# Attention steps of a fused kernel: transposes, drains and products with v one step later, other buffer counts, a smaller warm-up tile

## The chip, the cores and the metric

One core of one Trainium2 chip runs the whole program. The metric is the device time of one execution in microseconds. The kernel before takes 725.25 us, the median of three runs (724.98 to 725.36).

## The reference

Three parts follow one another, all in float32:

```python
# attention: B=2, H=8, S=576, D=64, scale = 1/8
cum = np.cumsum(np.maximum(s, 0.0), axis=-1)
bias = -(cum[:, :, :, None] - cum[:, :, None, :])
scores = np.where(causal, -1e9, scale * q @ k.T + np.minimum(bias, 0.0))
scores = scores - np.max(scores, axis=-1, keepdims=True)
attn = np.exp(scores)
attn = attn / (np.sum(attn, axis=-1, keepdims=True) + 1e-09)
x = (attn @ v) laid out as [B*S, H*D]            # 1152 x 512

# experts: E=4, F=1024
p = domain_probs / (domain_probs.sum(-1, keepdims=True) + 1e-09)
out = sum(p[:, e:e+1] * (np.maximum(x @ w1[e], 0.0) @ w2[e]) for e in range(E))

# gated layer, 1536 wide
y = ((out @ w_a) * (out @ w_b)) @ w_out
```

## The kernel before

**The whole.** Nearly all products are made of three matmuls (line 281): each operand is split into a high part and a rest (`xh`, `xl`, `wh`, `wl`), and high by high, rest by high and high by rest add up in one PSUM tile. The program has three stretches. In the first 30 us it does the attention of the first 256 tokens (the head, lines 787 to 865), eight heads one after another; while it waits for data, `keep_warm` (line 732) gives TensorE matmuls on a tile of ones, `lull`, whose result nobody reads (line 736). From 30 to about 194 us the attention of the other tokens runs beside expert 0 on the first 256 tokens (plain float32 matmuls, line 1037) and beside expert 1. After that come the other experts and the gated layer, up to 724 us.

**The attention pipeline.** The rest of the attention is 24 jobs: three groups of tokens, `GROUPS` (0,2,5), (1,0,3) and (1,3,5), eight heads each. A job has one tile of 128 queries for each index in its range; `sc_6_2_4` is the scores of head 6, of the group that begins at tile 2, for tile 4 (a number behind it in the queues below tells buffers apart). The second and third group are batch 1's and begin at tiles 0 and 3, so `av_3_0` is head 3 of the second group. `seq` lists all (job, tile) pairs. Step n of `attn_work` (line 939) issues one phase for each of several pairs, so that a pair goes through the phases in successive steps:

- scores of pair n (`st_scores`, L627 and L628, PSUM tag `sc`, two buffers; more than 512 keys take two pieces);
- softmax of pair n-1 (`st_softmax`): VectorE adds the mask and finds the row's extreme, out of PSUM into a tile `e` (L638); ScalarE takes the exponential (L651). `e` has five buffers;
- division of pair n-2 (`st_norm`): ScalarE L657, VectorE's reciprocal L658, GpSimd's product L659;
- transposes of pair n-3 on TensorE (`st_transpose`, L670), 128 keys each, into PSUM tag `tr`, two buffers of up to four blocks. A tile with five blocks takes a buffer with four and then one with the fifth;
- drain of pair n-3 (`st_evac`): ScalarE copies `tr` to `eh` (L685), then VectorE writes the rest to `el` (L686). A `tr` buffer is free when L686 has read it;
- when the last tile of a job is at n-4, its product with v (`st_av`, L702, PSUM tag `av`, one buffer): `eh` and `el` by `vs`. ScalarE (L719) and VectorE (L720) take the result out, and every second head GpSimd helps to split it into `xh`, `xl`.

The same steps load the next jobs' q, k, v (SyncE queues, L587 to L607) and prepare them (`prep_job`: `qh` on ScalarE, `qb` on VectorE L595, `ks` on ScalarE and GpSimd; `prep_v`: `vs`, two buffers).

**What sets the order.** The products of the experts are called in units, and `advance()` between them calls as many attention steps as a pace wants: for each group of tokens `lead` has the step by which the group must be through, `ends` (the last step of the group plus five), and the time of the stage by which it must be, 15 us ahead of the stage that reads the group's tokens. The written order is only a wish: a scheduler places every instruction in its engine's queue, and manual dependencies (`passed`) hold the experts' matmuls behind the attention steps. On the engine the queue is then fixed.

**Buffers.** Pool `h` holds the experts' hidden tiles (`hh`, `hl`, eleven buffers of each tag), pool `e` the tiles of the softmax.

Of the kernel before, what the change touches and what calls it, by code (L numbers as in the profile page):

```python
# [10 lines left out]
BF16 = mybir.dt.bfloat16  # L11
# [9 lines left out]
P = 128  # L21
NC = DM // P
SL = 512
# [14 lines left out]
GROUPS = [(0, 0, 2), (0, 2, 5), (1, 0, 3), (1, 3, 5)]  # L38
# [21 lines left out]
def fused_kernel(ctx, tc, qk0, v0, qT, kT, v, s, dp, w1, w2, wa, wb, wo, out):  # L60
    nc = tc.nc
# [21 lines left out]
    def open_pools(c, names):  # L83
        for name, bufs in names:
            pools[name] = c.enter_context(tc.tile_pool(name=name, bufs=bufs))
# [430 lines left out]


    actx = ExitStack()
    open_pools(actx, [("h", 11), ("raw", 3)])
    fix_p = actx.enter_context(tc.tile_pool(name="fix", bufs=1))  # L520
    causal = fix_p.tile([P, S], F32, name="causal")

# [1 line left out]
    qbs = [fix_p.tile([RB, 3 * P], F32R, name=f"qb{m}") for m in range(2)]  # L524
    rw_p = actx.enter_context(tc.tile_pool(name="rw", bufs=1))
    io_p = actx.enter_context(tc.tile_pool(name="io", bufs=2))
    e_p = actx.enter_context(tc.tile_pool(name="e", bufs=5))
    et_p = actx.enter_context(tc.tile_pool(name="et", bufs=2))
    st_p = actx.enter_context(tc.tile_pool(name="st", bufs=8))
    x_p = actx.enter_context(tc.tile_pool(name="x", bufs=1))  # L530
# [20 lines left out]
    def in_order(ins):  # L551
        return tc.keep_in_program_order(ins)
# [27 lines left out]
    def load_job(j):  # L580
        b, h = j.b, j.h
        j.qh = io_p.tile([P, j.nq], F32R, tag="qh", name=f"qh{j.nm}")
        j.qb = qbs[(j.h + 1) % 2]
        j.qr = rw_p.tile([P, j.nq], F32, tag="qr", name=f"qr{j.nm}")
        j.kr = rw_p.tile([P, j.nk], F32, tag="kr", name=f"kr{j.nm}")
        j.kb = io_p.tile([RB, j.nk], F32R, tag="kb", name=f"kb{j.nm}")
        queued(nc.sync.dma_start(out=j.qr, in_=qT[b, h, :, j.q0 : j.q1]))  # L587
        queued(nc.sync.dma_start(out=j.kr, in_=kT[b, h, :, : j.nk]))
        queued(nc.sync.dma_start(out=j.kb[D:, :].bitcast(F32), in_=ckD[:, PLACE[j.gi], h, : j.nk]))

    def prep_job(j):
        j.t = {}
        j.ks = io_p.tile([P, j.nk], F32R, tag="ks", name=f"ks{j.nm}")
        nc.scalar.activation(out=j.qh, in_=j.qr, func=AF.Copy, scale=SCALE)
        nc.vector.scalar_tensor_tensor(  # L595
            out=j.qb[:D, : j.nq], in0=j.qr[:D], scalar=SCALE, in1=j.qh[:D].bitcast(F32),
            op0=ALU.mult, op1=ALU.subtract,
        )
        nc.scalar.activation(out=j.ks, in_=j.kr, func=AF.Copy)
        queued(nc.sync.dma_start(out=j.kb[:D].bitcast(F32), in_=j.ks[:D].bitcast(F32)))  # L600
        nc.gpsimd.tensor_tensor(
            out=j.ks[D:, :], in0=j.kr[D:, :], in1=j.ks[D:, :].bitcast(F32), op=ALU.subtract
        )
# [11 lines left out]
    def st_enter(j, i):  # L615
        j.t[i] = Job()
        j.t[i].n = j.tiles[i][0] + P
# [36 lines left out]
    def st_norm(j, i):  # L654
        t = j.t[i]
        r = st_p.tile([P, 1], F32, tag="r", name="r")
        nc.scalar.activation(out=t.l, in_=t.l, func=AF.Copy, bias=1e-9)  # L657
        nc.vector.reciprocal(out=r, in_=t.l)  # L658
        nc.gpsimd.tensor_scalar(  # L659
            out=t.e, in0=t.e, scalar1=r, scalar2=1.0, op0=ALU.mult, op1=ALU.mult  # L660
        )
# [64 lines left out]

    lull = fix_p.tile([P, SL], BF16, name="lull")
    nc.gpsimd.memset(lull, 1.0)  # L730
    lull_ps = ps_m.tile([P, SL], F32, tag="mm", name="lullps")

    def keep_warm(n):

        for _ in range(n):
            in_order(nc.tensor.matmul(lull_ps, lhsT=lull[:, :P], rhs=lull, start=True, stop=True))  # L736

    sc = e_p.tile([NS, S], F32, tag="e", name="s_sb")
    ones = e_p.tile([P, S], F32, tag="e", name="ones")
# [15 lines left out]
    early[0] = False  # L755

    keep_warm(12)
    nc.vector.memset(ones, 1.0)
    nc.gpsimd.memset(sel_, 0.0)
# [167 lines left out]
    seq = [(j, i) for j in jobs for i in range(j.i0, j.i1)]  # L927
    state = {"n": 0}

    def at(n):  # L930
        return seq[n] if 0 <= n < len(seq) else None
# [7 lines left out]
    def attn_work(n):  # L939
        state["n"] += 1  # L940
        passed.append([])

        if x := at(n):
            j, i = x
            if i == j.i0:
                k = jobs.index(j)
                if k + 1 < len(jobs):
                    prep_job(jobs[k + 1])
                if k + 2 < len(jobs):
                    load_job(jobs[k + 2])  # L950
            st_enter(j, i)
        if x := at(n - 3):
            st_transpose(*x)
        if x := at(n):
            st_scores(*x)
        if x := at(n - 2):
            st_norm(*x)
        if x := at(n - 1):
            st_softmax(*x)
        if x := at(n - 4):  # L960
            j, i = x
            if i == j.i1 - 1:
                st_av(j)
        if x := at(n - 3):
            st_evac(*x)
        if x := at(n):
            j, i = x
            if i == j.i0:
                prep_v(j)
                k = jobs.index(j)  # L970
                if k + 1 < len(jobs):
                    load_v(jobs[k + 1])


    ends = [0] + [
        max(n for n, (j, i) in enumerate(seq) if j.gi == g) + 5 for g in range(1, len(GROUPS))
    ]

    late_ps = []
# [287 lines left out]
    n = [k for k, u in enumerate(after) if u[0] == ("w1", halves[1][1])][-1]  # L1267
# [12 lines left out]
    for n in range(len(seq) + 12):  # L1280
        x = at(n)
# [108 lines left out]
```

## Time and profile before

| | |
|---|---|
| median of three runs | 725.25 us (724.98 to 725.36) |
| the profiled execution's own time | 725.65 us |
| its span in the profile | 723.9 us |
| TensorE busy | 710.9 us (98%) |
| VectorE, ScalarE, GpSimd busy | 512.9, 323.5, 398.8 us |
| granted clock of TensorE | 1.000 of full speed |
| chain that ended last | TensorE 76%, VectorE 9%, GpSimd 5%, ScalarE 4% |

The span is what the profiler sees of the program from its first to its last instruction; the execution's own time is 1.75 us longer. TensorE is the fullest engine. Its busy time counts pipelined matmuls, whose ends are modelled, so a place is read from the starts of neighbouring matmuls and from the idle time that stands in brackets, with what released the engine.

### The profile page before, as it was taken

To read this page: it belongs to the slowest core of one execution; us is meant where nothing else is said; L and a number is where in the kernel's file an instruction comes from. 1 tells how busy PE (TensorE), PEld (TensorE's weight loads), DVE (VectorE), ACT (ScalarE), POOL (GpSimd) and SP (SyncE) were. 2 spreads that over 40 slices of the span, in tenths; PEclk is the share of its full clock that TensorE was granted. 3 is DMA by queue.
4 is the path that set the end of the run, shared out by engine and by line. 5 is a ranking of instruction groups with operands and counts; after the bars stand their busy time and mean duration, and the time that the engine had idled before them with its cause. 6 is when DMAs were issued, how large, how long until landed. Compare 5 with 4: busy or idle time off the path is not lost.

```text
span 723.9 us, 10979 instructions
## 1 busy us (share of the span) xinstructions
PE 710.9 (98%) x3884; PEld 620.9 (86%) x3886; DVE 512.9 (71%) x1060; ACT 323.5 (45%) x722; POOL 398.8 (55%) x329
## 2 busy tenths in 40 slices
PE   9999999999999999999999999999999999999998
PEld 5886798999899888888888888887999888888886
DVE  5586878767686866765655666589973969787674
ACT  3597899877434333331223123334544424243410
POOL 5476866655235544430333057687277879788600
PEclk9999999999999999999999999999999999999999
DMA  8665434442111211120111021222021222212003
GB/s 328 209 176 141 126 88 119 124 120 62 57 41 58 89 58 58 59 65 24 58 59 47 13 88 59 88 87 88 30 87 59 88 88 83 92 60 88 1 0 131
DMA packets 33724, 61.42 MB, mean 85 GB/s; under 512 B 3285, under 2 KB 17525, under 8 KB 33669
## 3 DMA queue, kind: packets, MB, share of 16 engines
q1 hardware_dynamic: 33189, 59.61, 26.6%
q10 hardware_dynamic: 480, 1.11, 0.4%
q8 instruction: 31, 0.51, 0.3%
q14 instruction: 24, 0.20, 0.1%
HBM read 55.11 MB, written 2.58 MB: 80 GB/s over the span
## 4 chain that ended last, share of the span: by engine, by line
PE 76%; DVE 9%; POOL 5%; issue 4%; ACT 4%; DMA 3%; SPq 0%; POOLq 0%; ACTq 0%; DVEq 0%
PE ps L281 34%; PE psq L281 24%; PE pst L281 6%; PE av L702 2%; PE tr L670 2%; POOL wl L81 2%; PE ps L1037 2%; DMA raw<-in_wo 1%; DVE el L686 1%; DVE tp L174 1%; PE lullps L736 1%; ACT e L651 1%; DVE h2l L81 1%; DVE tp L170 1%; POOL tp L162 1%
## 5 line engine op out<-in xcount | busy, mean ns | idle before, releaser
L281 PE MATMUL ps<-wh,h2h 128*128 128x512 f32 (+1 forms) x334 | 131.1, 392 | 0.6 <-ACT h2h L80 0.6
L281 PE MATMUL ps<-wl,h2h 128*128 128x512 f32 (+1 forms) x334 | 129.9, 389 | 0.0
L81 POOL TENSOR_TENSOR wl<-raw,wh 128x1024 fp32r<-128x1024 f32 x24 | 58.2, 2433 | 129.0 <-ACT wh L80 98.6
L281 PE MATMUL ps<-wh,h2l 128*128 128x512 f32 (+1 forms) x334 | 125.6, 390 | 0.0
L335 DVE SCALAR_TENSOR_TENSOR acc<-ps,pr,acc 128x512 f32<-128x512 f32 x111 | 82.3, 746 | 41.1 <-PE ps L281 40.4
L281 PE MATMUL psq<-xh,wh 128*128 128x448 f32 (+1 forms) x224 | 81.7, 365 | 0.1
L281 PE MATMUL psq<-xh,wl 128*128 128x448 f32 (+1 forms) x224 | 81.4, 363 | 0.0
L281 PE MATMUL psq<-xl,wh 128*128 128x448 f32 (+1 forms) x224 | 81.3, 363 | 0.0
L281 PEld LDWEIGHTS ps<-wh,h2l 128*128 128x128 f32 x334 | 62.7, 188 | 13.2
L281 PEld LDWEIGHTS ps<-wh,h2h 128*128 128x128 f32 x334 | 62.8, 188 | 13.0 <-ACT h2h L80 1.3
L346 ACT ACTIVATE h2h<-psq 128x448 fp32r<-128x448 f32 (+1 forms) x56 | 29.5, 530 | 95.5 <-PE psq L281 76.4
L281 PEld LDWEIGHTS ps<-wl,h2h 128*128 128x128 f32 x334 | 62.8, 188 | 10.9
L81 POOL TENSOR_TENSOR wl<-sums,wh 128x1024 fp32r<-128x1024 f32 x24 | 58.3, 2427 | 4.9 <-ACT wh L80 4.9
L80 ACT ACTIVATE wh<-raw 128x1024 fp32r<-128x1024 f32 x24 | 25.5, 1062 | 69.6 <-PE ps L281 53.0
L281 PE MATMUL psq<-tqh,wh 128*128 128x448 f32 x144 | 53.0, 368 | 1.3 <-DVE h2l L81 0.9
L281 PE MATMUL psq<-tql,wh 128*128 128x448 f32 x144 | 52.6, 365 | 0.0
L281 PE MATMUL psq<-tqh,wl 128*128 128x448 f32 x144 | 52.5, 364 | 0.0
L162 POOL TENSOR_SCALAR tp<-tp 128x512 f32<-128x512 f32 x24 | 48.0, 2017 | 5.8 <-ACT tp L161 5.8
L686 DVE TENSOR_TENSOR el<-tr,eh 128x512 fp32r<-128x512 f32 (+5 forms) x80 | 38.3, 484 | 16.4 <-ACT eh L685 15.6
L659 POOL TENSOR_SCALAR e<-e,r 128x448 f32<-128x448 f32 (+4 forms) x64 | 37.8, 595 | 17.5 <-DVE r L658 12.9
L281 PEld LDWEIGHTS psq<-xh,wh 128*128 128x128 f32 x224 | 42.1, 188 | 4.3 <-ACT s L445 0.9
L281 PEld LDWEIGHTS psq<-xl,wh 128*128 128x128 f32 x224 | 42.1, 188 | 3.5
(205 smaller groups left out, 1877.2 us busy)
## 6 DMA issues: line engine op xcount, KB each, us to landing
raw<-in_w SPq DMA_DIRECT2D x32, 512.0 KB
raw<-in_wa SPq DMA_DIRECT2D x12, 512.0 KB
raw<-in_wb SPq DMA_DIRECT2D x12, 512.0 KB
raw<-in_wo SPq DMA_DIRECT2D x12, 512.0 KB
kr<-in_kT SPq DMA_DIRECT2D x16, 288.0 KB
w<-in_w SPq DMA_DIRECT2D x8, 512.0 KB
vr<-in_v SPq DMA_DIRECT2D x16, 160.0 KB
kb<-ks SPq DMA_DIRECT2D x16, 144.0 KB
```

Source lines behind the costliest of these rows:

```text
L80: nc.scalar.activation(out=hi, in_=src, func=AF.Copy)
L81: lo_eng.tensor_tensor(out=lo, in0=src, in1=hi.bitcast(F32), op=ALU.subtract)
L162: nc.gpsimd.tensor_scalar(out=t.bitcast(F32), in0=t.bitcast(F32), scalar1=2.0**-15, scalar2=GMAX, op0=ALU.max, op1=ALU.min,)
L170: nc.vector.scalar_tensor_tensor(out=t, in0=lo, scalar=29, in1=t, op0=ALU.logical_shift_right, op1=ALU.bitwise_or,)
L281: ins = nc.tensor.matmul(ps, lhsT=l, rhs=r, start=first and k == 0, stop=last and k == 2, skip_group_check=more)
L335: nc.vector.scalar_tensor_tensor(out=dst, in0=ps, scalar=share, in1=dst, op0=ALU.mult, op1=ALU.add)
L346: nc.scalar.activation(out=hh, in_=src, func=AF.Relu)
L659: nc.gpsimd.tensor_scalar(out=t.e, in0=t.e, scalar1=r, scalar2=1.0, op0=ALU.mult, op1=ALU.mult)
L670: ins = nc.tensor.transpose(ps[:, c - c0, :], t.e[:, k0 : k0 + P], ident)
L686: nc.vector.tensor_tensor(out=j.el[:, c0:c1, x], in0=src, in1=hi.bitcast(F32), op=ALU.subtract)
L702: ins = nc.tensor.matmul(ps[:, o:], lhsT=j.vs[:, c, :], rhs=e[:, c, o:], start=(m == 0), stop=(m == len(mms) - 1),)
L1037: ins = nc.tensor.matmul(ps, lhsT=w, rhs=x, start=start, stop=stop)
```

## The change

It does five things:

1. `st_transpose` and `st_evac` are called for pair n-4, no longer n-3; `st_av` for a job whose last tile is n-5, no longer n-4. Scores, softmax and division stay where they were.
2. `ends` counts six steps behind a group's last pair, no longer five.
3. `e` has six buffers for five.
4. `h` has ten buffers for eleven.
5. `lull` is 128 columns wide for 512; the matmul reads these 128 columns four times through a broadcast, so it has the same shape (128 x 512) as before.

```diff
-    open_pools(actx, [("h", 11), ("raw", 3)])
+    open_pools(actx, [("h", 10), ("raw", 3)])
...
-    e_p = actx.enter_context(tc.tile_pool(name="e", bufs=5))
+    e_p = actx.enter_context(tc.tile_pool(name="e", bufs=6))
...
-    lull = fix_p.tile([P, SL], BF16, name="lull")
+    lull = fix_p.tile([P, P], BF16, name="lull")
...
-            in_order(nc.tensor.matmul(lull_ps, lhsT=lull[:, :P], rhs=lull, start=True, stop=True))
+            in_order(nc.tensor.matmul(
+                lull_ps.rearrange("p (a b) -> p a b", b=P), lhsT=lull,
+                rhs=lull.unsqueeze(1).broadcast_to([P, SL // P, P]), start=True, stop=True,
+            ))
...
-        if x := at(n - 3):
+        if x := at(n - 4):
             st_transpose(*x)
...
-        if x := at(n - 4):
+        if x := at(n - 5):
             j, i = x
             if i == j.i1 - 1:
                 st_av(j)
-        if x := at(n - 3):
+        if x := at(n - 4):
             st_evac(*x)
...
-        max(n for n, (j, i) in enumerate(seq) if j.gi == g) + 5 for g in range(1, len(GROUPS))
+        max(n for n, (j, i) in enumerate(seq) if j.gi == g) + 6 for g in range(1, len(GROUPS))
```

Below line 735 the changed file's lines are three higher for the same code (L1037 is L1040). From the end of the attention on, TensorE's queue is the same row for row. Inside the attention the scheduler has laid it out anew, and three places show how.

TensorE at the first head of the first group, before. `tr_0_2_3` fills one `tr` buffer, `tr_0_2_4` the other with four blocks, and the fifth block needs the first one back. The matmuls into `ps` are expert 0's first layer, the `sc` rows the next head's scores.

```order
L670 MATMUL tr_0_2_3_573<-ident,e_0_2_3_520 128x128 x4
L1037 MATMUL ps_633<-ckr,w_117 128x256 x3
L627 MATMUL sc_1_2_4_611<-ks_1_2_468,qh_1_2_448 128x320
L628 MATMUL sc_1_2_4_611<-kb_1_2_451,qb_83 128x320
L670 MATMUL tr_0_2_4_604<-ident,e_0_2_4_551 128x128 x4
L627 MATMUL sc_1_2_4_614<-ks_1_2_468,qh_1_2_448 128x256
L628 MATMUL sc_1_2_4_614<-kb_1_2_451,qb_83 128x256
L670 MATMUL tr_0_2_4_609<-ident,e_0_2_4_551 128x128
```

The same place after the change:

```order
L670 MATMUL tr_0_2_3_596<-ident,e_0_2_3_519 128x128 x4
L1040 MATMUL ps_665<-ckr,w_117 128x256
L627 MATMUL sc_1_2_4_601<-ks_1_2_468,qh_1_2_448 128x320
L628 MATMUL sc_1_2_4_601<-kb_1_2_451,qb_83 128x320
L627 MATMUL sc_1_2_4_604<-ks_1_2_468,qh_1_2_448 128x256
L628 MATMUL sc_1_2_4_604<-kb_1_2_451,qb_83 128x256
L1040 MATMUL ps_665<-ckr,w_117 128x256
L1040 MATMUL ps_714<-ckr,w_117 128x256 x3
L670 MATMUL tr_0_2_4_633<-ident,e_0_2_4_547 128x128 x4
L627 MATMUL sc_2_2_2_640<-ks_2_2_527,qh_2_2_474 128x320
L628 MATMUL sc_2_2_2_640<-kb_2_2_477,qb_84 128x320
L670 MATMUL tr_0_2_4_638<-ident,e_0_2_4_547 128x128
```

Between the two fills of that buffer there stand now five matmuls of expert 0 for three, and the scores of `sc_2_2_2`, which were behind this place, have come in front of the fifth block.

TensorE at head 6 of the same group, before: the rows that lead to head 7's first transposes, `tr_7_2_2`, which take the buffer that `tr_6_2_4` with four blocks had. Ahead of these rows stand those four transposes, the two matmuls of `sc_0_0_2`, the fifth block's transpose and six more L281.

```order
L281 MATMUL ps_1427<-xh,wh 128x256
L281 MATMUL ps_1427<-xl,wh 128x256
L281 MATMUL ps_1427<-xh,wl 128x256
L627 MATMUL sc_1_0_0_1505<-ks_1_0_1365,qh_1_0_1231 128x128
L628 MATMUL sc_1_0_0_1505<-kb_1_0_1234,qb_83 128x128
L702 MATMUL av_6_2_1396<-eh_6_2_1271,vs_6_2_1160 128x320
L670 MATMUL tr_7_2_2_1378<-ident,e_7_2_2_1309 128x128 x3
```

After the change:

```order
L670 MATMUL tr_6_2_4_1364<-ident,e_6_2_4_1230 128x128 x4
L628 MATMUL sc_0_0_2_1451<-kb_0_0_1107,qb_84 128x320
L627 MATMUL sc_1_0_0_1488<-ks_1_0_1351,qh_1_0_1209 128x128
L628 MATMUL sc_1_0_0_1488<-kb_1_0_1212,qb_83 128x128
L670 MATMUL tr_6_2_4_1369<-ident,e_6_2_4_1230 128x128
L281 MATMUL ps_1439<-xh,wh 128x256
L281 MATMUL ps_1439<-xl,wh 128x256
L281 MATMUL ps_1439<-xh,wl 128x256
L627 MATMUL sc_1_0_1_1522<-ks_1_0_1351,qh_1_0_1209 128x192
L628 MATMUL sc_1_0_1_1522<-kb_1_0_1212,qb_83 128x192
L702 MATMUL av_6_2_1413<-eh_6_2_1294,vs_6_2_1136 128x320
L670 MATMUL tr_7_2_2_1397<-ident,e_7_2_2_1274 128x128 x3
```

The nine L281 between the two uses have become three; the scores of `sc_1_0_0` and `sc_1_0_1` have come between instead.

VectorE's queue there, before, around the drain of `tr_6_2_4`:

```order
L638 ISA e_0_0_1_1473,mn<-sc_0_0_1_1436,causal 128x192
L638 ISA mn 128x1
L686 TENSOR_TENSOR el_6_2_1272<-tr_6_2_4_1336,eh_6_2_1271 128x4x128
L595 SCALAR_TENSOR_TENSOR qb_84<-qr_2_0_1372,qh_2_0_1371 64x320
L658 RECIPROCAL r<-l 128x1
L686 TENSOR_TENSOR el_6_2_1272<-tr_6_2_4_1341,eh_6_2_1271 128x128
```

and after:

```order
L658 RECIPROCAL r<-l 128x1
L638 ISA e_0_0_2_1495,mn<-sc_0_0_2_1451,causal 128x320
L638 ISA mn 128x1
L595 SCALAR_TENSOR_TENSOR qb_84<-qr_2_0_1358,qh_2_0_1357 64x320
L686 TENSOR_TENSOR el_6_2_1295<-tr_6_2_4_1364,eh_6_2_1294 128x4x128
L686 TENSOR_TENSOR el_6_2_1295<-tr_6_2_4_1369,eh_6_2_1294 128x128
```

The preparation `qb` stood behind the drain of the four blocks and now stands ahead of it, and the softmax in front is that of `sc_0_0_2` (320 keys), no longer of `sc_0_0_1` (192 keys).

TensorE at head 3 of the second group, where `av_3_0` needs what the last tile's transposes, `tr_3_0_2`, leave in `eh` and `el`, before:

```order
L670 MATMUL tr_3_0_2_1887<-ident,e_3_0_2_1836 128x128 x3
L281 MATMUL ps_1789<-wh,hh 128x512
L281 MATMUL ps_1789<-wl,hh 128x512
L281 MATMUL ps_1789<-wh,hl 128x512
L281 MATMUL ps_1789<-wh,hh 128x512
L281 MATMUL ps_1789<-wl,hh 128x512
L281 MATMUL ps_1789<-wh,hl 128x512
L627 MATMUL sc_5_0_2_1982<-ks_5_0_1814,qh_5_0_1715 128x320
L628 MATMUL sc_5_0_2_1982<-kb_5_0_1718,qb_83 128x320
L670 MATMUL tr_4_0_0_1918<-ident,e_4_0_0_1874 128x128
L627 MATMUL sc_6_0_0_2016<-ks_6_0_1905,qh_6_0_1820 128x128
L628 MATMUL sc_6_0_0_2016<-kb_6_0_1823,qb_84 128x128
```

After the change:

```order
L627 MATMUL sc_5_0_2_1973<-ks_5_0_1805,qh_5_0_1698 128x320
L628 MATMUL sc_5_0_2_1973<-kb_5_0_1701,qb_83 128x320
L670 MATMUL tr_3_0_2_1909<-ident,e_3_0_2_1829 128x128 x3
L627 MATMUL sc_6_0_0_2004<-ks_6_0_1896,qh_6_0_1811 128x128
L628 MATMUL sc_6_0_0_2004<-kb_6_0_1814,qb_84 128x128
L670 MATMUL tr_4_0_0_1935<-ident,e_4_0_0_1853 128x128
L627 MATMUL sc_6_0_1_2028<-ks_6_0_1896,qh_6_0_1811 128x192
L628 MATMUL sc_6_0_1_2028<-kb_6_0_1814,qb_84 128x192
L702 MATMUL av_3_0_1949<-eh_3_0_1869,vs_3_0_1723 128x320
L627 MATMUL sc_6_0_2_2066<-ks_6_0_1896,qh_6_0_1811 128x320
L628 MATMUL sc_6_0_2_2066<-kb_6_0_1814,qb_84 128x320
L702 MATMUL av_3_0_1949<-el_3_0_1870,vs_3_0_1723 128x320
```

Before, `av_3_0` came in the row behind these; after, the product with `eh` is the ninth row and that with `el` the last. Six L281 of expert 1 stood between the transposes and the product with v; none does now, and scores have taken part of their place.

## Rows read from the trace of the kernel before

**Rows 1.** Two stretches: us, length, then busy us (instructions) by engine, granted clock, DMA share
```profile
30.00:194.00 164.00, 157.69 (x1052) 139.41 (x1051) 119.78 (x392) 134.13 (x412) 105.06 (x131) 1.00 0.40 112
194.00:724.00 530.00, 524.76 (x2673) 461.33 (x2671) 377.21 (x608) 176.38 (x279) 278.51 (x161) 1.00 0.20 65
```

**Rows 2.** TensorE's waits, 30 to 195 us: releaser, total us, times, longest
```profile
PE tr L670 <- DVE el L686: 2.1, 6, 0.6
PE tr L670 <- DVE r L658: 1.3, 2, 0.7
PE av L702 <- DVE el L686: 1.2, 3, 0.8
PE sc L627 <- DVE mn L638: 1.0, 1, 1.0
PE av L702 <- ACT eh L685: 0.4, 1, 0.4
```

**Rows 3.** Timeline near 50 us: start, duration, what, [idle before <-releaser]
```profile
49.79 0.67 DVE L686 TENSOR_TENSOR el<-tr,eh 128x512 fp32r<-128x512 f32 x1
...
50.39 0.14 DVE L658 RECIPROCAL r<-l 128x1 f32<-128x1 f32 x1
...
50.60 0.30 PE L670 MATMUL tr<-ident,e 128*128 128x128 f32 x1 [0.70 <-DVE r L658]
```

**Rows 4.** Timeline near 182 us: one block of four transposes and its drain
```profile
182.11 0.63 PE L670 MATMUL tr<-ident,e 128*128 128x128 f32 x4 [0.63 <-DVE r L658]
...
182.50 0.36 PE L702 MATMUL av<-el,vs 128*128 128x256 f32 x1
...
182.78 0.60 ACT L685 ACTIVATE eh<-tr 128x512 fp32r<-128x512 f32 x1 [0.22 <-PE tr L670]
...
183.41 0.69 DVE L686 TENSOR_TENSOR el<-tr,eh 128x512 fp32r<-128x512 f32 x1 [0.65 <-ACT eh L685]
```

**Rows 5.** TensorE's timeline: five of its waits in their places
```profile
41.72 0.33 PE L670 MATMUL tr<-ident,e 128*128 128x128 f32 x1 [0.59 <-DVE el L686]
...
71.34 0.39 PE L627 MATMUL sc<-ks,qh 128*128 128x256 f32 x1 [0.98 <-DVE mn L638]
...
84.74 0.63 PE L670 MATMUL tr<-ident,e 128*128 128x128 f32 x4 [0.35 <-DVE el L686]
...
86.05 0.33 PE L670 MATMUL tr<-ident,e 128*128 128x128 f32 x1 [0.26 <-DVE el L686]
...
112.37 0.41 PE L702 MATMUL av<-el,vs 128*128 128x320 f32 x1 [0.81 <-DVE el L686]
```

**Rows 6.** Groups by form, 30 to 195 us: busy us, mean ns | idle before
```profile
L638 DVE CUSTOM_DVE_ANT_0 e<-sc,causal 128x320 f32<-128x320 f32 x32 | 15.4, 480 | 2.5 <-PE sc L628 1.8 <-PE tr L670 0.4
...
L595 DVE SCALAR_TENSOR_TENSOR qb<-qr,qh 64x320 fp32r<-64x320 f32 x8 | 5.3, 663 | 0.0
...
L686 DVE TENSOR_TENSOR el<-tr,eh 128x384 fp32r<-128x384 f32 x8 | 4.5, 557 | 1.7 <-ACT eh L685 1.6
...
L685 ACT ACTIVATE eh<-tr 128x384 fp32r<-128x384 f32 x8 | 3.8, 476 | 0.0
```

**Rows 7.** Line 595: duration in ns, least, median, longest; first and last start, forms
```profile
L595 DVE SCALAR_TENSOR_TENSOR qb<-qr,qh x24: 411/547/1569, 26.6 to 171.3; 64x384 fp32r<-64x384 f32 x8, 64x320 fp32r<-64x320 f32 x8, 64x256 fp32r<-64x256 f32 x8
```

**Rows 8.** Chain of waits: start, duration, run of matmuls on TensorE
```profile
55.70 2.58 PE ps L1037 x6
...
86.38 1.75 PE ps L281 x15
```

**Rows 9.** Timeline of the first 7 us
```profile
0.80 0.52 POOL L730 MEMSET lull<- 128x512 bf16 x1 [0.29 <-POOLq L1376]
...
1.38 5.30 PE L736 MATMUL lullps<-lull 128*128 128x512 bf16 x12 [1.38 <-POOL self L759]
...
1.81 0.20 POOL masks.py:197 MEMSET ident<- 128x128 f32 x1
...
6.61 0.46 PE L797 MATMUL sc<-cb,sel 40*128 40x128 f32 x1
```

## The prediction

> **What bounds it now.** I read the table by stretches first, then TensorE's waits between 30 and 195 us, then the timeline around each of those waits, then durations by form. The reader is to see that TensorE runs without a break where the kernel spends most of its time: 524.76 of 530 us behind the attention, at the full granted clock [rows 1], and its queue there is unchanged. So a shift that the attention makes is carried to the end, whole. In the 164 us of the attention TensorE is busy 157.69 [rows 1], and its waits for another engine sum to 6.0 us [rows 2]. That is all that a better pipeline could give; what a worse one costs has no such bound.
>
> Which waits are they? The list names L658, the reciprocal, for 1.3 us. That reading is wrong, and the timeline shows it: the fifth block's transpose starts at 50.60, the `el` of the block that had its buffer ends at 49.79 + 0.67 = 50.46, and the reciprocal at 50.39 merely ended last [rows 3]. So 3.4 us are waits for a `tr` buffer to be drained, 1.6 us (1.2 and 0.4) waits of the product with v for `el` and `eh`, and 1.0 us one wait of scores for an `sc` buffer [rows 2]. Not one waits for a normalised `e`. The extra step puts more work between division and transposes, where no wait was; the drain and the product move by the same step, so their distance is set anew only by the order of the queues.
>
> **The measure of a drain.** Four transposes start at 182.11 and the next matmul at 182.50, so a block takes 0.1; `eh` starts at 182.78, `el` at 183.41 and ends 0.69 later, at 184.10 [rows 4]. With 0.14 from there to the next transpose [rows 3] a buffer is ready 1.75 us after its last transpose. Work of TensorE between two uses of a buffer that falls short of 1.75 is waited for. Split matmuls run back to back at 1.75 / 15 = 0.117 for 256 columns, so 0.06, 0.09 and 0.145 for 128, 192 and 320; plain float32 matmuls leave two records each, 2.58 / 6 = 0.43 a record of 512 columns, so 0.43 for an instruction of 256 [rows 8].
>
> **Part by part.**
>
> *The small tile.* Its fill takes 0.52, and the matmuls start behind it at 1.38; the identity's, of as many bytes as the new tile, takes 0.20 [rows 9]. The scores follow the last warm-up matmul, whose run ends at 6.68 [rows 9]. So the head starts 0.32 earlier at most, and at least not at all if a load sets it. I take **-0.2** (0 to -0.32), nearer the row that shows scores right behind the run.
>
> *Buffers.* None of TensorE's waits is for a free buffer of `e` or `h` [rows 2], so the sixth `e` gives nothing by itself; it holds the tile that lives a step longer. The tenth `h` costs nothing while the plain expert's second layer takes tiles as fast as the first makes them. `vs` is now read a step later, and the loads of v stand some rows later in SyncE's queue, behind those of q and k; TensorE waits for none of them [rows 2]. All this **0**; if that cover went, it would be a wait of the product with v.
>
> *Fifth blocks.* Waits of 0.59, 0.35 and 0.26 [rows 5] and the 0.70 of [rows 3] stand in the first group where the new queue puts more between. The first place shown goes from three plain matmuls, four transposes and two pairs of scores, 1.29 + 0.4 + 0.29 + 0.23 = 2.2 us, to 3.4. There the drain was late by more than my measure: 2.2 + 0.59 - 1.75 = 1.05 us, VectorE being in something else. All four gone is -1.9; if half that lateness meets other places, -0.6. I take **-1.5**.
>
> *Heads 4 to 7 of the first group, and the next head.* Here the first transposes of a head move closer to the four blocks ahead of them. In the second place shown there were 0.29 + 0.1 + nine of 0.117 + 0.12 + 0.145 = 1.7; now 0.145 + 0.12 + 0.1 + 0.35 + 0.18 + 0.145 = 1.04, short by 0.7. Counted the same way, heads 4 and 5 have 1.62 (short by 0.13 each), head 6 and head 0 of the next group 1.24 (0.5 each). Sum 2.0, against 0.1 before: **+1.9**. It is +0.9 if each drain is 0.2 quicker than [rows 4]. It is +3.2 with VectorE's queue: at head 7 the softmax of 320 keys (0.48) and `qb` (0.66) [rows 6] now stand ahead of `el`. These scores end 0.54 after the first transpose, so `el` starts at 1.68 or later, against 1.30 in [rows 4]: 0.4 more, and as much again at two like places.
>
> *The second group's product with v.* `el` of three blocks is there 0.28 + 0.476 + 0.03 + 0.557 + 0.14 = 1.48 us after the last transpose (the two means from [rows 6], the lags from [rows 3, 4]). In the third place shown there were over 2 us of work; now 0.12 + 0.1 + 0.18 + 0.145 + 0.29 = 0.84, short by 0.64. Head 4 is the same, heads 0 and 2 have 1.20 and 1.24 (0.26 each): 1.8. Such waits cost 1.2 before [rows 2], 0.81 of it at one place [rows 5], though the count gives 0.1, so lateness of VectorE comes on top. I take 2.2 for 1.2: **+1.0** (-0.2 if `eh` and `el` are each 0.1 quicker at four places; +2.1 with all the old lateness).
>
> *The tail.* Before, one short distance (0.9) made the 0.63 of [rows 4]; now two are short, 0.9 and 1.26, by 0.85 and 0.5: **+0.3** (-0.2 to +0.8).
>
> *The wait of scores,* 0.98 [rows 5]: its short distance (0.44) goes, but six others under 0.6 come. **0**, from -0.98 to +1.0.
>
> Sum: -0.2 - 1.5 + 1.9 + 1.0 + 0.3 = +1.5. The profiled execution took 725.65 and would take 727.15; the median stands 0.4 lower, at 725.25, so I say **726.8 us**. The ends do not meet all at once; this case by itself I give 725.0 to 729.2.
>
> **A rule against the change.** `qb` takes 0.41 us at best and 1.57 at worst for tiles of 256 to 384 columns [rows 7]: something holds it up. The Trainium skill's page "SBUF — State Buffer", section "Who interferes with whom", says that a VectorE instruction with two inputs in SBUF contends with a GpSimd instruction that reads SBUF, and that the one which is second waits for the whole of the other. By that rule the spread is GpSimd's doing, and `qb` ahead of a drain would cost up to the difference of these two figures; this trace agrees with the spread, and whether GpSimd makes it no row here proves. What it would do to the time is the second rival.
>
> **Rivals.**
>
> *Faster, about 722.2.* The four late drains go in full (-1.9), the scores' wait too (-0.98), the warm-up gives its 0.2, and the places that I count as short are not: TensorE's real spacing between kinds of matmul is wider than back to back, or `eh` comes sooner. For it: the waits of before hardly followed my count (1.0 us counted in `tr` waits, 3.4 there), so lateness rules, and a step more may absorb it. Against: where a gap was shortest, the count was near (0.85 counted, 0.63 seen [rows 4]).
>
> *Slower, about 729.5: `qb` ahead of the drain.* In three places of the new order `qb` stands ahead of an `el` for which TensorE soon waits (heads 6 of the first, 3 and 4 of the second group); before, it stood behind it in these. At 1.57 for the mean of 0.66 [rows 6, 7] each costs 0.9 more, 2.7 in all over my sum. It decides from where `qb` takes over about 0.9 there. Against: the median over all 24 is 0.55 [rows 7].
>
> *No change, about 725.0.* The moved waits are the same waits elsewhere: TensorE is ahead of its drains by what the experts' work allows, and the order only picks where it stops; the warm-up's 0.2 is what is left.
>
> **How the numbers follow.** About 0.2%, 1.45 us, can be told from no change: below 723.8 is faster, above 726.7 slower. My case has 0.52, with slightly more than half of it above 726.7 (0.28 slower, 0.23 same, 0.01 faster). Faster rival 0.21 (0.20 faster, 0.01 same), `qb` 0.15 (slower), no change 0.12 (same). So 0.21 faster, 0.36 same, 0.43 slower. The range of 722.6 to 729.3 leaves out some half of the faster rival and of the `qb` case, which is 0.18.
>
> **What would show it.** Right: the sum of TensorE's waits in the attention grows from 6.0 to 7.5 or 8; waits of `tr` for `el` stand at the first transposes of heads 4 to 7 and leave the fifth blocks of heads 0 and 1; waits of `av` for `el` stand at heads 0, 2, 3 and 4 of the second group; busy time behind the attention as before, and the first scores some 0.2 to 0.3 earlier. Wrong: waits of `tr` below 2 us, a new wait for `e`, `vs` or `h`, or a change of time behind 194 us.

## The result: slower, by more than the range allowed

The changed kernel takes 733.71 us (median of six runs, 731.61 to 736.41), the kernel before 725.31 in the same comparison: a ratio of 1.0118, 95% interval 1.0104 to 1.0131. That is 8.4 us more, where 1.5 was forecast; the time lies above the range. The direction and the place (the attention) were right, the size was not. Some executions, of the kernel before as of others, took 11 to 13 us longer at a mean clock near 0.98; they are left out of every comparison and median below.

The profiled execution took 736.41 us with a span of 734.7. The first matmul behind the attention (the first into `psq`) starts at 215.35, before at 204.26: 11.1 us later, and the whole span is 10.8 longer. All of the time is lost ahead of that point. Two stretches after the change, to be held against [rows 1]:

```profile
30.00:205.00 175.00, 165.04 (x1050) 142.91 (x1051) 122.04 (x392) 136.87 (x411) 105.52 (x131) 0.98 0.38 105
205.00:735.00 530.00, 524.92 (x2673) 461.51 (x2671) 377.24 (x608) 176.67 (x279) 278.42 (x161) 1.00 0.20 65
```

Behind the attention TensorE is as busy as before, 524.92 of 530. Inside it there are two things that [rows 1] does not have: more waiting, and a granted clock of 0.98 where it was 1.00.

**The waits.** TensorE's waits in the attention, the same view as [rows 2]:

```profile
PE tr L670 <- DVE el L686: 2.9, 5, 1.6
PE sc L627 <- DVE mn L638: 2.9, 7, 0.7
PE av L702 <- ACT eh L685: 2.7, 4, 1.5
PE sc L628 <- DMA kb<-ks: 0.9, 1, 0.9
PE tr L670 <- DVE r L658: 0.4, 2, 0.2
```

They sum to 9.8 us for 6.0. The waits of scores for line 638, which empties the `sc` buffers, have grown from 1.0 (one) to 2.9 (seven); the product's waits for `eh` from 0.4 to 2.7; a wait for a load is new. The product's waits for `el`, 1.2 before, are not in the list any more.

This list tells too little: a matmul's end is modelled and can cover the start of a wait, and the waits grow by 3.8 us where 11.1 are lost. The weight loads, which are a row of their own in the profile (PEld), stop for the same releasers and show more of a wait. For 95 to 140 us, about the second group of tokens, before:

```profile
PEld av L702 <- DVE el L686: 1.9, 3, 1.0
PEld tr L670 <- PE sc L628: 0.3, 1, 0.3
PEld av L702 <- ACT eh L685: 0.2, 1, 0.2
```

and after:

```profile
PEld sc L627 <- DVE mn L638: 3.8, 7, 1.0
PEld av L702 <- ACT eh L685: 1.7, 1, 1.7
...
PEld av L702 <- DVE el L686: 0.6, 3, 0.2
```

From 2.4 us to over 6, where TensorE's own list has 1.2 and 4.5 in the same stretch.

The starts of the matmuls give an estimate that needs no modelled end. For each form, take the spacing to the next start that a quarter of its kind keep below in the kernel before, and add up what the spacings between the pipeline's first scores and the first matmul into `psq` have beyond it. This sum grows by 11.3 us: by 4.3 where the next row is a score that waits for line 638 (from 1.2 to 5.5), by 1.4 at products with v, by 1.0 at the load, by 0.3 at transposes; the rest is at no named wait, and the clock is in it.

**The clock.** TensorE's granted clock in stretches of 4 us around the two falls (columns as in [rows 1], the clock is the number behind POOL's count):

```profile
114.00:118.00 4.00, 2.91 (x17) 2.15 (x16) 3.91 (x15) 3.89 (x14) 0.79 (x2) 0.98 0.33 96
118.00:122.00 4.00, 4.00 (x15) 3.19 (x14) 1.89 (x8) 2.42 (x9) 2.92 (x5) 0.59 0.47 132
...
130.00:134.00 4.00, 2.33 (x13) 1.64 (x11) 2.35 (x9) 2.31 (x9) 0.70 (x1) 1.00 0.26 70
134.00:138.00 4.00, 3.95 (x15) 3.41 (x16) 2.60 (x11) 3.46 (x14) 3.57 (x6) 0.61 0.54 145
138.00:142.00 4.00, 4.00 (x21) 3.34 (x21) 1.76 (x6) 2.04 (x7) 2.28 (x3) 0.96 0.47 125
```

Twice TensorE had run thin, 2.91 of 4 us busy and then 2.33 of 4, and both times the lower of the two levels (1.2 GHz for 2.4) was granted for over 3 us after it. In stretches of 2 us the share of the clock that is missing sums to 3.4 us. So of the 11.1 us some 3.4 are the clock. Most of the rest stands at the named waits, 7.1 by the estimate from the starts.

A fall of the clock is not the changed kernel's alone. The small tile alone (experiment 1) leaves TensorE's queue as it was before, and its profiled execution has a fall too, at 73 us, just after the wait of 0.98 that the scores have there as before:

```profile
68.00:72.00 4.00, 3.02 (x10) 1.56 (x10) 2.65 (x8) 4.00 (x11) 2.12 (x2) 1.00 0.54 138
72.00:76.00 4.00, 3.81 (x19) 3.53 (x19) 3.19 (x12) 3.18 (x11) 3.92 (x5) 0.64 0.69 203
```

Of 29 executions of the kernel before beside the first experiments eight had a mean clock of 0.997 or 0.998 and took 726.7 to 727.5 us; the others took 723.9 to 726.5.

**Where the longest waits stand.** Ten of TensorE's waits after the change, in the manner of [rows 5]:

```profile
71.44 0.30 PE L670 MATMUL tr<-ident,e 128*128 128x128 f32 x1 [1.64 <-DVE el L686]
...
91.22 0.52 PE L670 MATMUL tr<-ident,e 128*128 128x128 f32 x3 [0.23 <-DVE r L658]
...
96.51 0.35 PE L627 MATMUL sc<-ks,qh 128*128 128x192 f32 x1 [0.35 <-DVE mn L638]
...
97.75 0.52 PE L670 MATMUL tr<-ident,e 128*128 128x128 f32 x3 [0.40 <-DVE el L686]
...
109.14 0.36 PE L627 MATMUL sc<-ks,qh 128*128 128x192 f32 x1 [0.46 <-DVE mn L638]
...
114.89 0.35 PE L627 MATMUL sc<-ks,qh 128*128 128x192 f32 x1 [0.34 <-DVE mn L638]
...
116.46 0.41 PE L627 MATMUL sc<-ks,qh 128*128 128x320 f32 x1 [0.75 <-DVE mn L638]
...
134.05 0.41 PE L702 MATMUL av<-eh,vs 128*128 128x320 f32 x1 [1.49 <-ACT eh L685]
...
192.56 0.38 PE L702 MATMUL av<-eh,vs 128*128 128x256 f32 x1 [0.63 <-ACT eh L685]
193.29 0.66 PE L670 MATMUL tr<-ident,e 128*128 128x128 f32 x4 [0.34 <-DVE el L686]
```

By their place in the queue these are: the fifth block of `tr_3_2_4` (71.44); `tr_6_2_2` (91.22); `sc_1_0_1` (96.51); `tr_7_2_2` (97.75); `sc_3_0_1`, `sc_4_0_1` and `sc_4_0_2` (109.14 to 116.46); `av_4_0` (134.05); `av_5_3` and `tr_6_3_3` in the tail. The fifth blocks of heads 0 and 1 do not wait any more.

### The profile page after: what moved, and what is told of

Its sections match the earlier page's. It is cut to its first block, busy times and chain, and to the rows that moved or that the text cites. A ratio compares the mean times of both kernels' runs of the same rounds, so it can differ in the third digit from the quotient of the medians.

```text
span 734.7 us, 11018 instructions
## 1 busy us (share of the span) xinstructions
PE 718.0 (98%) x3886; PEld 624.2 (85%) x3886; DVE 515.1 (70%) x1060; ACT 326.9 (44%) x722; POOL 398.2 (54%) x329
## 4 chain that ended last, share of the span: by engine, by line
PE 73%; DVE 10%; POOL 5%; ACT 5%; issue 3%; DMA 3%; SPq 0%; ACTq 0%; POOLq 0%; DVEq 0%
PE ps L281 33%; PE psq L281 23%; PE pst L281 5%; PE av L702 3%; PE tr L670 2%; POOL wl L81 2%; PE ps L1040 2%; DVE h2l L81 1%; PE sc L627 1%; DVE tp L174 1%; PE sc L628 1%; DVE tp L170 1%; DMA raw<-in_wo 1%; ACT e L651 1%; DMA kr<-in_kT 1%
## 5 line engine op out<-in xcount | busy, mean ns | idle before, releaser
L281 PE MATMUL ps<-wh,h2h 128*128 128x512 f32 (+1 forms) x334 | 131.1, 393 | 0.6 <-ACT h2h L80 0.6
L281 PE MATMUL ps<-wl,h2h 128*128 128x512 f32 (+1 forms) x334 | 130.0, 389 | 0.0
L281 PE MATMUL ps<-wh,h2l 128*128 128x512 f32 (+1 forms) x334 | 125.6, 390 | 0.0
L281 PE MATMUL psq<-xh,wh 128*128 128x448 f32 (+1 forms) x224 | 81.7, 365 | 0.1
L281 PE MATMUL psq<-xh,wl 128*128 128x448 f32 (+1 forms) x224 | 81.4, 363 | 0.0
L281 PE MATMUL psq<-xl,wh 128*128 128x448 f32 (+1 forms) x224 | 81.3, 363 | 0.0
L281 PEld LDWEIGHTS ps<-wh,h2l 128*128 128x128 f32 x334 | 62.7, 188 | 13.3
L281 PEld LDWEIGHTS ps<-wh,h2h 128*128 128x128 f32 x334 | 62.8, 188 | 12.8 <-ACT h2h L80 1.2
L281 PEld LDWEIGHTS ps<-wl,h2h 128*128 128x128 f32 x334 | 62.8, 188 | 10.9
L281 PE MATMUL psq<-tqh,wh 128*128 128x448 f32 x144 | 53.0, 368 | 0.9 <-DVE u L436 0.4
L281 PE MATMUL psq<-tql,wh 128*128 128x448 f32 x144 | 52.6, 365 | 0.0
L281 PE MATMUL psq<-tqh,wl 128*128 128x448 f32 x144 | 52.5, 365 | 0.0
L281 PEld LDWEIGHTS psq<-xh,wh 128*128 128x128 f32 x224 | 42.1, 188 | 4.3 <-ACT s L445 0.9
L281 PEld LDWEIGHTS psq<-xl,wh 128*128 128x128 f32 x224 | 42.1, 188 | 3.5
```

The lines of the kernel that those rows point to most:

```text
L281: ins = nc.tensor.matmul(ps, lhsT=l, rhs=r, start=first and k == 0, stop=last and k == 2, skip_group_check=more)
```

## The experiments

Four questions: which of the five edits costs the time; whether they add up; what the longest wait is made of; and which of the moved phases does it.

**1. The edits one by one.** The small tile alone (`lull` at 128 columns, nothing else):

> The kernel before with the 128-column warm-up tile alone; every queue as before. Theory (the moved steps cost the time, through waits of TensorE in the attention and a lower clock behind the longest of them): 725.0 to 725.3, that is 0 to 0.3 less than before, waits as before (6.0 us). Rival (the tile, read four times over, slows the warm-up or starts the attention in another phase): 727 or more.

Measured 0.9994 (0.9978 to 1.0011): nothing that can be told. What it does at the start is seen in the changed kernel, whose rows these are:

```profile
0.80 0.20 POOL L730 MEMSET lull<- 128x128 bf16 x1 [0.29 <-POOLq L1379]
...
5.78 0.32 PE L800 MATMUL sc<-cb,sel 40*128 40x128 f32 x1
...
30.58 0.63 PE L628 MATMUL sc<-kb,qb 67*128 67x320 f32 x2 [0.85 <-DMA kb<-ks]
```

In the changed kernel the fill takes 0.20, the first scores of the head start at 5.78 for 6.61 [rows 9], and the first scores of the pipeline at 29.02. Their second matmul then waits 0.85 for `kb`, a load that was issued at 27.00 (27.22 before). The gain ends at that load: this second matmul starts at 30.58, in the kernel before at 30.20. The run with the pace alone, below, has the same wait, of 1.22, without being slower. With the small tile alone the head starts at 5.61 and the pipeline's first scores at 30.60, later than the 29.67 of before.

The buffers without the moved steps (this diff and the next ones are cut short):

```diff
-("h", 11)          +("h", 10)
-name="e", bufs=5   +name="e", bufs=6
(and the small tile)
```

> The kernel before with the small tile, six buffers of e and ten of h; the steps stay where they were. Theory: 725 +- 1.5, no clock below full. Rival (the buffer counts, by the other order that they make the scheduler choose, cost the time): 730 or more, with the clock low for some us.

Measured 1.0005 (0.9988 to 1.0022). The buffers alone cost nothing that can be told.

The moved steps with the old buffers and the old tile (`n - 4`, `n - 5`, `n - 4`, `+ 6`):

> The kernel before with the steps moved (transposes and drains n-4, product n-5, ends + 6), five buffers of e and eleven of h, old tile. Theory: about as slow as the changed kernel, 731 to 736, clock below 1.000 in some runs. Rival (the buffer counts): 725 to 727.

Measured 1.0052 (1.0036 to 1.0069), 729.13 us. Neither expectation: slower, but only by half. And the pace alone:

```diff
-    ... if j.gi == g) + 5 for g in ...
+    ... if j.gi == g) + 6 for g in ...
```

> The kernel before with ends + 6 alone: one more attention step is packed into each stage ahead of its deadline. Theory: 725 to 727. Rival (the pace costs the time, not the later drain): 730 or more.

Measured 0.9982 (0.9969 to 0.9994): if anything faster; between executions with a clock of 0.999 or 1.000 it is 0.4 us, 724.42 for 724.82. So the moved steps, with the pace that goes with them, cost some 4 us with five buffers of `e`, and the sixth buffer, free by itself, costs another 3 to 4 together with them. No run moves the steps without the pace.

**2. The sixth buffer together with the moved steps.** The changed kernel with `e` back at five:

> The changed kernel with five buffers of e for six, all else as changed; TensorE's queue is that of the run with the old buffers. Theory (the sixth buffer with the moved steps lets the scheduler bunch the scores, which then wait for the two sc buffers): 728 to 731, TensorE's and its weight loads' waits for L638 near those of before (1 to 2 us) where the changed kernel has 5.0. Rival (the buffer is harmless, the steps cost it all): 732 to 735.

Measured 1.0072 (1.0048 to 1.0096), 728.59 us. TensorE's waits in the attention:

```profile
PE tr L670 <- DVE el L686: 3.1, 9, 0.5
PE av L702 <- ACT eh L685: 2.7, 3, 1.4
PE sc L627 <- DVE mn L638: 0.5, 2, 0.3
```

The scores' waits for L638 are down to 0.5 (for 2.9), in the weight loads' list to 0.4 (for 5.0): with five buffers the scores nearly always find an `sc` buffer empty. I take it that the wait for a free `e` keeps the scheduler from bunching them, which no run shows by itself. The drains and the products with v wait as much as in the changed kernel. So the sixth buffer's part is in the main the scores'; the wait for `kb` (0.9) is gone as well.

**3. The long wait for `eh`.** The product `av_4_0` waits 1.49 us at 134.05. ScalarE's timeline of the changed kernel shows why:

```profile
132.49 0.68 ACT L599 ACTIVATE ks<-kr 128x576 fp32r<-128x576 f32 x1 [1.69 <-DMA kr<-in_kT]
...
133.53 0.58 ACT L685 ACTIVATE eh<-tr 128x384 fp32r<-128x384 f32 x2
```

The drain `eh` (L685) is behind the preparation of k (L599) in ScalarE's queue, and that one waits 1.69 us for its load. SyncE issued this load at 127.95, right behind that of q:

```profile
127.24 0.52 SPq L587 DMA_DIRECT2D qr<-in_qT  x1
127.95 0.33 SPq L588 DMA_DIRECT2D kr<-in_kT  x1
```

ScalarE could go on 4.5 us after that. In the kernel before it started 3.0 us after the issue of the same load (125.99 for 123.01), and 3.0 from 127.95 would have been 130.95, when ScalarE had just come free (130.80). So the load was not late, it was long. The packets of the transfers, between 128 and 132.4, show one thing beside the loads:

```profile
q8 instruction: 1, 0.02, 2.4%
```

This is one packet of 16 KB, from 129.15 on, for 1.70 us. Of 131 packets of the load's row size (2304 bytes; the load has 128) 123 had started by 130.25; the last eight, a sixteenth of the load, started one after another from 130.84, when that packet was through, to 131.93. In experiment 5 the same is seen with a packet of 1.01 us. That it held up the eight is inferred from their times; no run takes it away.

I had taken the ring of v's buffers to be the origin, and gave `vs` a third buffer, in a pool of its own (`h` at nine for the room, which leaves every queue as it is; some 20 of TensorE's 3600 rows move by the third buffer):

> The changed kernel with a third buffer of vs (room for it from a ninth buffer of h, which alone leaves every queue as it is). With the product one step later, the split of v for the job after next has to wait for it, the load of the next v waits for that, and the loads of q and k stand behind it in SyncE's queue. Theory (this chain makes ScalarE wait 1.7 us for k in front of a drain, near 132 us): that wait is gone, no product with v waits over 1 us for eh, 729 to 732. Rival (the chain is only one delay among many, and other waits take its place): 732.5 to 735.

Measured 1.0088 (1.0070 to 1.0105), 730.56 us, the clock at 0.999 or 1.000 in all four runs. Its waits (the attention's lines are one higher there):

```profile
PE tr L671 <- DVE el L687: 2.2, 6, 0.6
PE sc L628 <- DVE mn L639: 1.9, 6, 0.7
PE av L703 <- ACT eh L686: 0.9, 2, 0.6
PE av L703 <- DVE el L687: 0.7, 1, 0.7
```

No product waits over 0.7 us, the load of `kb` costs 0.2, and no transposes wait over 0.6; the scores still wait 1.9. ScalarE does not wait for this job's k any more: the load is issued at 125.19, no packet of the queue `q8 instruction` falls into it, and the preparation starts at 128.25. ScalarE waits 1.13 us for the next job's k instead, and no drain of which TensorE is in need stands behind that. So the time came out as expected, some 2 us less than the changed kernel's (1.0088 for 1.0118). But the mechanism that I gave for it (v's loads hold up k's) is not shown: SyncE's loads of v wait for the split of v by 25.2 us in all in the kernel before and by 25.2 in the changed one.

Both remedies together:

> The changed kernel with five buffers of e and three of vs. Theory (two causes, each with its own part): 726 to 728.5. Rival (the drain's distance itself, which neither mends): 728.5 to 731, as with five e alone.

Measured 1.0067 (1.0048 to 1.0087): the rival's number. They do not add. And the third buffer where the steps stay:

> The kernel before with ends + 6, small tile, ten h and a third vs; the steps stay. If v's ring cost something with the old steps too: 722.5 to 724. If not: 724 to 725, as with ends + 6 alone.

Measured 1.0012 (0.9979 to 1.0044), 726.20 us: no gain at all, rather a loss beside the 0.9982 of the pace alone. Both forms of my expectation were too low. With the old steps, and with five buffers of `e`, the third buffer gives nothing; that fits an order that fell out better rather than a buffer that was missing, but for the changed kernel no run tells the two apart.

**4. Which moved phase.** The product with v alone one step later:

```diff
-        if x := at(n - 4):      # st_av
+        if x := at(n - 5):
```

> The kernel before with the product with v alone one step later (n-5) and ends + 6; transposes and drains at n-3, old buffers. ends + 6 alone gave 0.9982 of before. If what is left with five e (1.007) comes of the product's new step (v's buffers held longer, the product beside another tile's scores): 1.004 or more, 727.5 to 730. If it comes of the moved transposes and drains: 0.998 to 1.002, 723.5 to 726.

Measured 1.0023 (1.0010 to 1.0035): between the two, near the second. Transposes and drains later, with the product behind the drain in the same step, where it was:

```diff
-        if x := at(n - 3):      # st_transpose
+        if x := at(n - 4):
...
-        if x := at(n - 4):      # st_av
-        if x := at(n - 3):      # st_evac
+        if x := at(n - 4):      # st_evac
+        if x := at(n - 4):      # st_av
```

> The kernel before with transposes and drains one step later (n-4), ends + 6, and the product with v right behind the drain in the same step (n-4, where it was); old buffers. If the moved transposes and drains cost the time: 1.004 or more, 727.5 to 731; the product now also waits for its last drain, so more than in the changed order is possible. If the product's step did: 0.998 to 1.002.

Measured 1.0091 (1.0066 to 1.0116). Beside the pace alone (0.9982), which both runs contain, the product's step costs 0.4%, that of the transposes and drains 1.1%, and both together, above, only 0.7%. Here the drain's distance to the product is shorter as well, as the expectation says. So each of the two moves costs by itself, they do not add up, and no share of the loss can be given to either.

**5. The changed kernel again.**

> The changed kernel itself, beside the two others on one chip: 1.010 to 1.013 of before. With the third vs it was 1.0088 at a clock of 1.000 in all its runs; if the low clock behind the long wait near 134 us is what the third vs takes away, the clock here is below 1.000 again in half of the runs or more.

Measured 1.0117 (1.0080 to 1.0154). The profiled execution of this run had a clock of 1.000 throughout and a span of 731.0, still 7.1 more than before. Its waits stand at the same places (1.64 at `tr_3_2_4`, 1.27 at `av_4_0`). By the estimate from the starts the spacings have 7.9 us more than before, 6.9 of them at named waits: 3.5 at scores for L638, 1.6 at the load of `kb`, 1.3 at products, 0.6 at transposes. So at full clock the loss is waits, and the scores' are the most. The thin stretches are there too:

```profile
113.00:117.00 4.00, 2.84 (x14) 1.94 (x13) 3.94 (x14) 3.89 (x15) 0.31 (x2) 1.00 0.39 109
117.00:121.00 4.00, 4.00 (x27) 3.51 (x26) 3.37 (x16) 3.84 (x16) 3.73 (x7) 1.00 0.39 110
...
128.00:132.00 4.00, 2.50 (x14) 1.78 (x13) 2.57 (x10) 2.54 (x10) 0.92 (x2) 1.00 0.29 85
132.00:136.00 4.00, 4.00 (x23) 3.42 (x24) 2.37 (x9) 3.60 (x14) 3.45 (x6) 1.00 0.54 145
```

2.84 and 2.50 of 4 us busy, and no fall behind either. So the thin stretch is where the clock can fall, not where it must. One of the three executions that are compared had a clock below 0.999 (0.995), fewer than the half that was expected; with four executions of the third `vs` at 0.999 or 1.000 beside it, whether that buffer takes the falls away stays open.

**6. A third `sc` buffer.** Taken from the experts' accumulators (`ps_s` 3, `ps_m` 2), in both kernels:

> The kernel before with three buffers of sc and two PSUM accumulators for the experts in place of three. A control: whatever the loss of an accumulator costs is in both. One wait of scores (0.98) can go: 724 to 726 if two accumulators are enough, more if not.

> The changed kernel with the same. If the shortage of sc buffers is a cause of its own: no wait of scores for L638 between 95 and 140 us, and 2.5 to 4.5 us less between this and the control than the 9 between the changed kernel and the one before. If the delay only shows there: still 7 or more above the control, with the waits at transposes or products.

Measured 1.0313 (1.0268 to 1.0359) and 1.0294 (1.0277 to 1.0310). The lost accumulator costs 22 us and lowers the clock in both, also behind the attention (0.98 between 400 and 600 us). The weight loads' waits for L638 between 95 and 140 us, in the kernel before and in the changed one, both with three `sc` buffers:

```profile
PEld sc L627 <- DVE mn L638: 2.1, 3, 1.5
...
PEld sc L627 <- DVE mn L638: 0.3, 1, 0.3
```

In the changed kernel the scores' waits are gone with the third buffer (0.3 for 3.8; TensorE's own list has none), as the first of the two cases of the expectation has it, and the two kernels are level, where it left 4.5 to 6.5 us between them. That fits a shortage of `sc` as a cause of its own. What it is worth in time is not settled: the clock of these executions runs from 0.980 to 0.995, and other waits of the changed kernel have grown (3.6 us at transposes for 2.9).

**7. A version that is better than both.** Pace and small tile alone:

> The kernel before with ends + 6 and the small tile, nothing else: 723.5 to 725, 0.997 to 0.999 of before, if the 0.9982 of ends + 6 alone was no chance; 0.9995 to 1.0005 if it was.

Measured 0.9978 (0.9957 to 0.9999), 723.86 us: faster than the kernel before by just more than its uncertainty, and not to be told from the pace alone (0.9982), whose queue on TensorE it has.

## Why the prediction was wrong

**Right.** What bounds the kernel: time moved in the attention alone and was carried to the end whole. That the reciprocal was a false name, and the drain of `tr` the true one. That buffers of `e` and `h` give nothing by themselves: 1.0005. That the pipeline would be slower for a denser second group, and that ten `h` cost nothing.

**The terms of the sum, one by one.**

- *Small tile, -0.2.* The head starts 0.83 us earlier, more than the 0.32 that the term gave at most, but a load (`kb`) is next and takes it all. The prediction had named this end of its range.
- *Fifth blocks, -1.5.* The four waits of 1.90 us are gone. One of 1.64 came at another fifth block, `tr_3_2_4`: VectorE was in two pieces of a weight split (L227), of which the second, at 68.47, took 1.76 us, and had a product's output in front of the drain. The last row is the duration of this line in the kernel before (ns: least, median, longest):

```profile
67.81 2.42 DVE L227 TENSOR_TENSOR wl<-raw,wh 128x512 fp32r<-128x512 f32 x2
...
68.47 1.76 DVE L227 TENSOR_TENSOR wl<-raw,wh 128x512 fp32r<-128x512 f32 x1
...
68.03 3.33 POOL L227 TENSOR_TENSOR wl<-raw,wh 128x512 fp32r<-128x512 f32 x2
...
70.16 0.47 DVE L720 TENSOR_TENSOR xs<-av,xt 64x320 f32<-64x320 f32 x1
...
70.63 0.66 DVE L686 TENSOR_TENSOR el<-tr,eh 128x512 fp32r<-128x512 f32 x1
...
L227 DVE TENSOR_TENSOR wl<-raw,wh x8: 679/688/1811, 46.7 to 111.2; 128x512 fp32r<-128x512 f32 x8
```

  GpSimd was in pieces of the same split for the whole of these 1.76 us. In the kernel before the one piece that had GpSimd's split beside it throughout took 1.81, and six of the other seven took 0.68 to 0.69. So some 1.1 of the 1.64 us go with GpSimd's split, by the difference to the median, an estimate. The Trainium skill's page "SBUF — State Buffer", section "Who interferes with whom", says that a VectorE instruction with two inputs in SBUF contends with a GpSimd instruction that reads SBUF. These durations agree with that; no run takes GpSimd away at this place to prove it. The prediction had said that lateness might meet another place; it took little of the gain back for that and should have taken nearly all.
- *Heads 4 to 7, +1.9.* Measured 0.23 and 0.40 at heads 6 and 7, nothing at the other three places. Distances counted in back-to-back matmuls named two places that waited and three that did not, and their sum was three times too dear.
- *The second group's product, +1.0 from waits for `el`.* **This step failed.** There is no wait for `el` left in TensorE's list there: 0 for the 2.2 of the sum. TensorE does stop in this dense block, as counted, but a row earlier: at the scores, which wait for `sc` buffers that the same VectorE empties. By the time that TensorE is through, `el` is there.
- *The wait of scores, 0.* **This step failed most.** The text counted six short distances and then let them cancel against one that goes. They cost 1.9 us more in TensorE's list, 3.8 in the weight loads' (5.0 for 1.2 between 20 and 205 us), 4.3 from start to start, and 3.5 of 7.9 in the execution at full clock; the range of the term ended at +1.0. The run with five buffers of `e` shows that, with the moved steps, it is the sixth buffer that puts the scores so close: there they wait 0.5.
- *Loads of q, k and v in SyncE's queue, 0.* Failed as well: 0.85 for `kb` at the start, and 1.69 of ScalarE's time for k, which became 1.49 of TensorE's. The reason given was that TensorE waited for no load before. But the chain goes through ScalarE's queue, where a preparation that waits for its load stands in front of a drain that is ready; ScalarE waited 2.1 us for k in the kernel before already, at four places. That one of these loads became so long is no fault of the count (experiment 3).
- *The tail, +0.3.* 1.29 us of waits for 1.48.
- *The clock.* Not in the text at all. In the profiled run it is 3.4 us, more than any term. Over the runs of the changed kernel it is less: those at 0.999 or 1.000 took 731.6 to 733.4, those at 0.998 took 734.0 and 734.2, that at 0.995 took 736.4. So about 7 of the 8.4 us are there without a fall of the clock: the median of the first three is 732.7, that of the kernel before 725.3.

**The rivals.** None came. The slower one, `qb` ahead of the drain, named a true kind of delay, a VectorE instruction in front of an `el`; but in the worst place it was the weight split, and none of its three places waited over 0.4 us for an `el`. What holds `qb` up, which the prediction left open, the two traces show. The longest after the change, with GpSimd's split of k beside it:

```profile
72.78 1.42 POOL L601 TENSOR_TENSOR ks<-kr,ks 64x576 fp32r<-64x576 f32 x1
...
72.80 1.81 DVE L595 SCALAR_TENSOR_TENSOR qb<-qr,qh 64x384 fp32r<-64x384 f32 x1
```

The seven `qb` that took over 0.9 us, three before and four after, all began while GpSimd was in a split (L601 or L227) with 0.62 to 1.40 us still to go, and ended 0.28 to 0.41 us after it. All that began with no GpSimd instruction under way took 0.41 to 0.55.

**The likeliest error.** I priced one engine's waits by distances and let each of the others be on time. Three of the four large waits have something in another engine's queue ahead of the work that TensorE needs: the weight split on VectorE (1.64, and 0.75 at `sc_4_0_2`, where it stands at 114.90 for 1.29 us) and the preparation of k on ScalarE (1.49). The fourth (0.85, `kb`) is a load that was issued as soon as its input was there.

**Left open.** What the shortage of `sc` buffers is worth in time. Whether k's load took 4.5 us for the one packet of 16 KB. What the moved steps cost without the pace. And why the orders that the scheduler makes from such small edits differ by some 4 us: the runs show which edits do, and that they do not add up.

## What to carry to other kernels

In a pipeline with fixed queues a later phase is not more slack: it is a new order on every engine, and its price is what stands in front of the work that the busiest engine waits for, on all of them. Count the short distances of every shared buffer, price them alike, and follow each load through the queue in which it is consumed. And put one edit in at a time: here the pace alone gained 0.2% at most, the buffers alone nothing, and the sixth buffer, free by itself, cost 3 to 4 us together with the moved steps.

## What the runs showed of the hardware that I had not expected

- TensorE's granted clock fell to its lower level for over 3 us at a time behind stretches in which it was busy for 2.91 and 2.33 of 4 us, and in another execution of the same program it did not (2.84 and 2.50 of 4 us busy, 1.00 after). It fell in the order of the kernel before as well (3.02 of 4 us busy, then 0.64).
- The weight loads' waits show more of the short stops than the matmuls' own (3.8 for 2.4 us of the scores' waits for L638 between 95 and 140 us).
- A piece of the weight split on VectorE that had the same split on GpSimd beside it throughout took 1.76 us after and 1.81 before, where the median is 0.69. Every `qb` over 0.9 us ended 0.28 to 0.41 us after a split on GpSimd that was under way when it began.
- While a packet of 16 KB of the queue `q8 instruction` was under way for 1.70 us, a load of 128 rows had all but its last eight packets started; these came one after another when it was through, and the load took 4.5 us for the 3.0 of before.
